# A new instruction order for packed attention with a SoLU layer: weight parts first, score and Z products in one run

## The chip, the cores and the metric

The kernel runs on one core of one Trainium2 chip. The core has TensorE (PE: matrix products into PSUM), VectorE (DVE), ScalarE (ACT), GpSimd (POOL) and SyncE (SP, which here only issues DMAs). The metric is the device time of one execution in microseconds; less is better. Three runs of the kernel before took 371.79 to 372.6 us, median 372.57 us.

## What is computed

```python
s = scale * np.matmul(qq, kk.transpose(0, 1, 3, 2)); s = s - np.max(s, axis=-1, keepdims=True)
a = np.exp(s); a = a / (np.sum(a, axis=-1, keepdims=True) + 1e-09)
sm_attn(qq, kk, vv) = np.matmul(a, vv)
p_packed = sm_attn(p, k, v)              # 32 packed rows per head
x = sm_attn(q, p_packed, p_packed)       # 8 batches, 8 heads, 576 rows, 64 wide
h = x @ w_in                             # (4608, 512) @ (512, 1024)
e = np.exp(h - h_max); sm = e / (np.sum(e, axis=-1, keepdims=True) + 1e-09)
solu = h * sm
ln = (solu - mu) / np.sqrt(var + 1e-06) * g_ln
out = ln @ w_out                         # (4608, 1024) @ (1024, 512)
```

The weights come as 64-bit words and are put together as float32 on the chip before use.

## The kernel before, in words

The work is written as some 1,120 small steps, and a table in the source, `ORDER`, names them in the order in which they are issued. Every engine takes its share of the steps in that order, first in, first out; SP's queue of DMAs too. A step is `name/batch` (attention, eight batches; `/w` for the weights) or `name-tile` (36 tiles of 128 output rows). Behind a colon stands a PSUM bank (0 to 7) or the engine (a = ScalarE, v = VectorE, p = GpSimd) where it can be chosen.

Weights: `lw0` to `lw3` load the four parts of w_in, `lW0` to `lW3` those of w_out, 1024 KB each. `wl` and `wa` take the two halves of each word, `wm` joins them on VectorE (L199). `wp`, `wb`, `pw`, `cs`, `cv`, `ct` find the scales and centre w_out; `ch` and `cl` split it into two float16 halves `wch` and `wcl`; `zw` and `zy` do so for w_in (`w_hi` and the rest). Until a weight part is joined its raw words lie in a buffer that `W_HOME` names.

Attention of a batch: `lk0`, `lk1` (704 and 576 KB), `lv` (1280 KB) and `lq0`, `lq1` (576 KB each) load; `s10`, `s11` are the products of p and K, `mx`, `mb`, `ex` their softmax, `tp`, `tc` (first three batches) or `eh`, `el`, `et`, `ea` the transpose; `av` is the product with V; `pp`, `pt`, `pc` scale and turn it. `sx0`, `sx1` are the scores of q, `sb`, `sm`, `su`, `se`, `ss`, `si`, `sr`, `sn`, `at`, `ah`, `al` their softmax up to the float16 halves `a2h` and `a2l`. `z0`, `z1` multiply the packed rows with w_in (Z = p_packed @ w_in, so that h = a2 @ Z): in float32 for batches below `Z16`, in three float16 terms from there on; `zh`, `zl` split Z into halves. `s1`, `sx` and `z` work on TensorE cut into tiles of 64 rows and 32 columns, `av` into 128 by 32, all others use the whole array.

A row tile i: `m1` is h (12 matmuls of 512 columns), then `nm`, `nb`, `bd`, `ex`, `u`, `mu`, `yh`, `yl`, `sq`, `ca`, `cr` on the other engines, `tr` (a transposing DMA from `yhl` to `yT`), `m2a` and `m2b` (12 matmuls each), `ev` (the scaled copy of the result to `o_sb`) and `st` (the store). Tiles 4, 13, 22 and 31 straddle two batches. An `m1` needs two PSUM banks, which `u` gives back. `m1` of a batch needs that batch's `al` and `zl`.

`hw` are pairs of matmuls whose result nobody reads. After tile 0 to 3 (batch 0) and their second products, the first tile that needs batch 1 follows.

Of the kernel before, what the change touches and what calls it, by code (L numbers as in the profile page):

```python
# [33 lines left out]
se0/0 wa1/w tc0/1:a ss0/0 si0/0:a wa3/w wm1/w hw2/w:1 tc1/1:a wp0/w:6 wp1/w wp2/w tp2/1:2 wl3/w:v sr0/0 sn0/0:p se1/0
wm3/w wp3/w at0/0 wb0/w wb1/w tc2/1:a ss1/0 wb/w z0/0:4 z1/0:0 si1/0:p sr1/0 sn1/0:p wl4/w:a wa4/w wm4/w wa6/w wl6/w:a
ri/1:p un/0 wm6/w ah0/0:a uq/0 wa5/w wl5/w:v wm5/w cs0/w:6 cs1/w wp4/w:7 lk0/2 cs4/w cs5/w cs2/w zh0/0:a zw3/w:p at1/0
cs3/w lk1/2 wp5/w s10/2:2 zl0/0 wl7/w:a wp6/w wa7/w rs/1 zh1/0:a wm7/w mx0/2 ah1/0:a lv/1 wp7/w pw0/w al0/0:p al1/0:p
s11/2:4 pw1/w zl1/0 lq0/1 lq1/1 pw/w mx1/2 cs6/w cs7/w cv/w:a mb0/2:a ko/w gd/w ct0/w ct1/w ct4/w mb1/2:a m1-1:0 ct5/w
nm-1 ex0/2 av/1:7 m1-2:2 lk0/3 bd-1:p ct2/w ex1/2 ri/2:p ch0/w:a pp/1:a ct3/w ct6/w ch2/w:a nb-1:a ch1/w:a cl1/w:p ex-1
ct7/w tp0/2:6 lv/2 nm-2 tc0/2:a bd-2:p u-1 m1-3:4 nm-3 nb-2:a ex-2 u-2 tp1/2:7 cl2/w:p pt/1:6 tc1/2:a pc/1:a yh-1:a  # L40
tp2/2:7 bd-3:p yl-1:p pe/1 s10/3:0 mu-1:a tc2/2:a mx0/3 sq-1 mb0/3:a sx0/1:2 sb0/1 ex0/3 rs/2 ch3/w:a pk/1 un/1 lk1/3
lk0/4 av/2:7 pp/2:v cl0/w:p sx1/1:2 sb1/1 ca-1 nb-3:a s11/3:0 mx1/3 ex-3 mb1/3:a pt/2:6 sm/1 m1-0:2 lq0/2 u-3 nm-0
su/1:p lk1/4 bd-0:p ex1/3 eh/3:a tr-1 lq1/2 yh-3:a yl-3:p nb-0:v z0/1:0 z1/1:4 cl3/w:v cr-1 se/1 tr-3 ss/1 m2a-1:7
zh0/1:a zl0/1 zh1/1:a lk0/5 el/3:p et/3 ex-0 pc/2:a zl1/1 si/1:a sr/1 m2b-1 ev-1:a s10/4:0 s11/4:4 u-0 yh-0:a mx0/4 ca-3
m2a-3:7 sn/1:v pe/2 yl-0:p pk/2 m2b-3 ca-2 mu-3:a mb0/4:a ex0/4 mu-2:a at/1 ah/1:a mx1/4 mb1/4:a al/1:v sx0/2:2 sb0/2
uq/1 sx1/2:0 ex1/4 un/2 sb1/2 ea/3:p ri/4:v m1-4:4 uc-4 nm-4 ri/3:a sm/2 eh/4:a zz/0 el/4:p bd-4:v zw1/w:a sq-3 cr-3
nb-4:v ex-4 yh-2:v yl-2:p mu-0:p sq-2 tr-0 m1-7:2 nm-7 ev-3:a u-4 st-1 ca-0 nb-7:a rs/3 lv/3 ex-7 bd-7:v lk1/5 lq0/3
zy1/w u-7 su/2:p yh-4:a m2a-0:6 mu-7:p m1-8:0 sq-0 cr-0 ca-7 s10/5:4 mx0/5 tr-2 av/3:7 zw2/w:a se/2 nm-8 mb0/5:a bd-8:p
lq1/3 yl-4:p m2b-0 ev-0:a st-3 zy3/w yh-7:a ex0/5 lv/4 m1-6:2 pp/3:v pt/3:7 uq/2 ss/2 si/2:p nm-6 nb-8:a m2a-2:6 ex-8
ca-8 s11/5:4 yl-7:v u-8 mu-8:v cr-2 sq-7 mu-4:a tr-7 sq-4 mx1/5 m2b-2 pe/3 ph/2:a nb-6:a ex-6 pk/3 zy2/w zw0/w:v ev-2:a  # L50
pl/2 zy0/w tr-4 bd-6:p m1-5:0 nm-5 et/4 pc/3:v mb1/5:a ex1/5 u-6 lk0/6 m2a-7:6 lk1/6 yh-8:a st-0 z0/2:4 z1/2:2 zh0/2:a
yl-8:p un/3 ph/3:a sq-8 sr/2 sn/2:v at/2 m2a-4:7 m2b-7 nb-5:a ea/4:v bd-5:p cr-7 m2b-4 uq/3 lk0/7 yh-6:v zh1/2:a zl1/2
sx0/3:2 st-2 mu-6:v ah/2:a al/2:p eh/5:a ex-5 u-5 zz/1 ev-7:a lq0/4 yl-6:p av/4:6 rs/4 zl0/2 sb0/3 sx1/3:0 el/5:p
# [5 lines left out]
yl-9:v sx0/4:2 tr-12 sb0/4 sx1/4:4 sb1/4 sm/4 su/4:v m1-13:0 nm-13 m2a-12:7 bd-13:v nb-13:v m1-11:2 nm-11 m2b-12 ex-13
yh-10:a u-13 yl-10:p sq-10 cr-12 mu-9:a sq-9 nb-11:v ex-11 lq0/5 eh/6:v tr-9 bd-11:v m1-14:4 tr-10 u-11 mu-11:a yh-11:v  # L60
ea/5:p se/4 nm-14 mu-13:a st-5 bd-14:v nb-14:v ex-14 el/6:p m2a-9:6 rs/5 yl-11:p lq1/5 av/5:0 pp/5:a ev-12:v m1-16:2
pe/5 cr-9 u-14 nm-16 m2b-9 m1-17:0 ca-11 m2a-10:7 et/6 nb-16:v st-12 ss/4 ph/4:a yh-13:v yl-13:v lv/6 nm-17 bd-17:v
tr-11 sq-13 ca-13 cr-13 sq-11 cr-11 ex-16 cr-10 lq0/6 bd-16:p m1-15:4 m2b-10 st-8 zz/2 tr-13 nb-17:v u-16 ex-17 u-17
si/4:v ev-10:a ca-17 pl/4 ea/6:v sr/4 sn/4:p ev-9:a st-9 z0/4:2 yh-16:v z1/4:0 at/4 st-10 zh0/4:a zl0/4 zh1/4:a zl1/4
m2a-11:7 mu-16:v pt/5:6 m2b-11 yl-16:v uq/4 ca-16 sq-16 cr-16 m2a-13:0 ev-11:a nm-15 nb-15:v tr-16 lk1/7 ah/4:v bd-15:p
ex-15 u-15 mu-15:v yh-15:v yl-15:p pk/5 al/4:v mu-17:p m2b-13 pc/5:v un/5 uq/5 m2a-16:7 st-11 rs/6 sx0/5:2 sq-15 ev-13:a
sx1/5:4 yh-14:v sb0/5 s10/7:0 s11/7:2 av/6:6 mx0/7 mb0/7:p sb1/5 sm/5 yl-14:p mu-14:a sq-14 tr-15 uc-22 m1-20:4 mx1/7
pp/6:a pe/6 pt/6:6 yh-17:a nm-20 ph/5:a lq1/6 pl/5 m2b-16 ex0/7 zz/3 mb1/7:a st-13 nb-20:a tr-14 m1-19:0 ex1/7 su/5:v
bd-20:p ex-20 u-20 pc/6:a se/5 ss/5 si/5:p pk/6 z0/5:2 z1/5:4 ev-16:a m2a-14:7 un/6 zh1/5:a ca-14 cr-14 nm-19 m2a-15:6
eh/7:a ca-15 el/7:p m2b-14 m2b-15 sr/5 bd-19:p sn/5:v at/5 ah/5:a zh0/5:v al/5:v zl0/5 zl1/5 m1-23:2 lv/7 et/7 yh-20:a  # L70
ev-14:a st-14 mu-20:p yl-20:v ea/7:v sx0/6:4 cr-15 yl-17:p tr-17 av/7:7 sq-20 sb0/6 nb-19:a ex-19 u-19 m1-22:4 nm-23
nb-23:v ev-15:a st-15 bd-23:p ri/7:a rs/7 pp/7:v sq-17 ex-23 sx1/6:0 nm-22 sb1/6 m2a-17:6 ca-19 ca-20 u-23 yh-23:v
mu-23:v tr-20 m2a-20:7 cr-20 nb-22:a yl-23:p sm/6 m1-24:0 nm-24 ex-22 ca-23 m2b-20 m1-21:2 bd-22:p m2b-17 sq-23 tr-23
# [826 lines left out]
```

## Time and profile before

| | us |
|---|---|
| median of three runs | 372.57 |
| the profiled execution | 372.9 |
| its span, first to last instruction | 371.1 |
| PE busy | 354.9 (96%) |
| DVE busy | 278.9 (75%) |
| ACT busy | 209.1 (56%) |
| POOL busy | 214.7 (58%) |

The profiled execution is 1.8 us longer than its span, and 0.33 us longer than the median. Busy times are sums over a program with unlike stages: the loads and the weights up to about 46 us, a stage up to about 80 us in which w_out is still being split while tiles 0 to 3 run, and the long rest. Matmul rows begin every 0.216 us where TensorE does not wait, though each lasts 0.38 us, since they are pipelined.

### The profile page before, as it was taken

The numbers are of one execution on the slowest core, as the hardware profiler recorded it, in microseconds if no ns is written. First come the engines' busy times: TensorE is split into PE (matmuls) and PEld (weight loads), VectorE is DVE, ScalarE is ACT, GpSimd is POOL, SyncE is SP. The second block draws the span as 40 slices with busy tenths as digits, with TensorE's granted clock in tenths as the row PEclk, the third lists the DMA queues.
The fourth block names the chain that finished last, engine by engine and source line by source line (L and its number), as shares of the span: only waits on it lengthen the run. The fifth ranks groups of instructions, "written<-read, shape, count | busy, mean of one in ns | idle before, by whom it ended". The sixth has DMA issues, their size and how long they took to land.

```text
span 371.1 us, 7650 instructions
## 1 busy us (share of the span) xinstructions
PE 354.9 (96%) x3027; PEld 165.9 (45%) x3027; DVE 278.9 (75%) x421; ACT 209.1 (56%) x357; POOL 214.7 (58%) x304
## 2 busy tenths in 40 slices
...
GB/s 284 425 422 419 425 382 68 126 266 284 229 191 325 227 171 157 153 150 258 156 212 171 198 115 124 44 97 150 148 115 164 92 113 59 113 141 54 148 170 58
DMA packets 99349, 70.57 MB, mean 190 GB/s; under 512 B 88048, under 2 KB 88048, under 8 KB 97776
## 3 DMA queue, kind: packets, MB, share of 16 engines
...
q8 instruction: 24, 0.39, 0.4%
q14 instruction: 13, 0.11, 0.1%
HBM read 38.80 MB, written 9.44 MB: 130 GB/s over the span
## 4 chain that ended last, share of the span: by engine, by line
PE 83%; DVE 7%; DMA 6%; POOL 3%; issue 1%; ACT 0%; SPq 0%; POOLq 0%
PE pa L789 41%; PE ps L723 23%; PE ps L789 8%; DMA qT<-in_q_dram 4%; PE ps L604 3%; PE ps L538 2%; PE pa L316 1%; PE pa L504 1%; DMA zh<-in_moe_w_in_dram 1%; POOL wcl L329 1%; PE ps L436 1%; DVE u L752 1%; DVE zl L622 1%; DVE nm L729 1%; DVE yT L323 1%; POOL s L586 1%
## 5 line engine op out<-in xcount | busy, mean ns | idle before, releaser
L789 PE MATMUL pa<-wch,yT 128*128 128x512 f16 x480 | 149.5, 379 | 0.8 <-ACT yhl L148 0.8
L789 PEld LDWEIGHTS <-yT 128*128 128x128 f16 x864 | 83.2, 98 | 104.5 <-issue 4.8
L789 PE MATMUL pa<-wcl,yT 128*128 128x512 f16 x240 | 91.0, 379 | 0.0
L729 DVE TENSOR_REDUCE nm<-ps 128x1 f32<-128x1024 f32 x36 | 43.9, 1220 | 29.1 <-PE ps L723 28.9
L763 POOL TENSOR_TENSOR yhl<-u,yhl 128x1024 f16<-128x1024 f32 x23 | 51.2, 2227 | 21.2 <-ACT yhl L148 9.8
L747 ACT ACTIVATE e<-ps,bias,unit 128x1024 f32<-128x1024 f32 x36 | 43.3, 1202 | 35.4 <-DVE bias L144 28.5
L723 PE MATMUL ps<-zh,a2h 128*128 128x512 f16 (+1 forms) x160 | 54.8, 380 | 0.1
L752 DVE SCALAR_TENSOR_TENSOR u<-e,s_row,ps 128x1024 f32<-128x1024 f32 x36 | 45.6, 1267 | 12.2 <-ACT e L747 9.6
L723 PE MATMUL ps<-zh,a2l 128*128 128x512 f16 (+1 forms) x160 | 54.6, 379 | 0.0
L723 PE MATMUL ps<-zl,a2h 128*128 128x512 f16 (+1 forms) x160 | 54.6, 379 | 0.0
L771 ACT ACTIVATE e<-u,negmu 128x1024 f32<-128x1024 f32 x36 | 41.1, 1143 | 8.0 <-DVE negmu L144 7.8
L723 PEld LDWEIGHTS <-a2h 128*128 128x128 f16 (+1 forms) x320 | 27.7, 100 | 33.9 <-issue 3.1
L740 POOL TENSOR_SCALAR bound<-nm,unit 128x1 f32<-128x1 f32 x22 | 18.9, 859 | 27.1 <-DVE nm L729 27.0
L789 PE MATMUL ps<-wch,yT 128*128 128x512 f16 x96 | 30.2, 379 | 0.0
L142 ACT ACTIVATE o_sb<-pa,c_row 128x512 f32<-128x512 f32 x22 | 14.9, 684 | 25.9 <-POOL c_row L782 9.2
L148 ACT CAST yhl<-u 128x1024 f16<-128x1024 f32 x20 | 20.7, 1041 | 15.3 <-DVE u L752 13.0
L781 POOL TENSOR_SCALAR c_row<-sq,k_out,s_eps 128x1 f32<-128x1 f32 x36 | 14.8, 411 | 20.1 <-ACT e L771 19.4
L782 POOL TENSOR_TENSOR c_row<-c_row,neg_half 128x1 f32<-128x1 f32 x36 | 22.3, 619 | 3.0
L775 POOL TENSOR_SCALAR s_eps<-se,s_row 128x1 f32<-128x1 f32 x36 | 14.5, 402 | 15.3 <-ACT e L747 12.2
L723 PEld LDWEIGHTS <-a2l 128*128 128x128 f16 (+1 forms) x160 | 14.3, 100 | 16.8
L763 DVE TENSOR_TENSOR yhl<-u,yhl 128x1024 f16<-128x1024 f32 x13 | 17.6, 1354 | 2.3 <-ACT yhl L148 2.2
L789 PE MATMUL ps<-wcl,yT 128*128 128x512 f16 x48 | 18.2, 379 | 0.0
...
## 6 DMA issues: line engine op xcount, KB each, us to landing
...
```

The source lines that it names most:

```text
L142: nc.scalar.activation(out, in_, AF.Copy, scale=scale)
L148: nc.scalar.copy(out, in_)
L723: nc.tensor.matmul(h[rows, 512 * n:512 * n + 512], lhsT=lhsT, rhs=z[:, r, 512 * n:512 * n + 512], start=t == 0, stop=t == end)
L729: nc.vector.tensor_reduce(out=nm, in_=st['h'], axis=AX.X, op=ALU.max, negate=True)
L740: eng.tensor_scalar(out=bound, in0=st['nm'], scalar1=st['nm'], scalar2=st['unit'][:, 2:3], op0=ALU.mult, op1=ALU.max)
L747: nc.scalar.activation(st['e'], st['h'], AF.Exp, bias=st['bias'], scale=st['unit'][:, 1:2], accum_out=st['se'])
L752: nc.vector.scalar_tensor_tensor(out=st['u'], in0=st['e'], scalar=st['s_row'], in1=st['h'], op0=ALU.mult, op1=ALU.mult, accum_out=st['su'])
L763: engines[on(f'yl-{i}', 'v')].tensor_tensor(out=st['y'][:, 1], in0=st['u'], in1=st['y'][:, 0], op=ALU.subtract)
L771: nc.scalar.activation(st['e'], st['u'], AF.Square, bias=st['negmu'], accum_out=st['sq'])
L781: nc.gpsimd.tensor_scalar(out=c_row, in0=st['sq'], scalar1=k_out[:, 0:1], scalar2=s_eps, op0=ALU.mult, op1=ALU.add)
L782: nc.gpsimd.tensor_tensor(out=c_row, in0=c_row, in1=neg_half, op=ALU.pow)
L789: nc.tensor.matmul(st['po'], lhsT=st['yT'][:, a, c], rhs=w[:, c], start=c == 0 and t == 0, stop=c == NFC - 1 and t == 2)
```

## The change

The table `ORDER` is new as a whole, with 1,115 steps in place of 1,120. Beside it four edits stand:

```diff
-Z16 = 2
+Z16 = 3
-W_HOME = 'zh zl zh zl kT qT v zh'.split()
+W_HOME = 'zh w_hi zh wcl kT qT v wch'.split()
     def stage(home):
-        if home in ('zh', 'zl'):
+        if home in ('w_hi', 'wcl', 'wch'):
+            return {'w_hi': w_hi, 'wcl': wcl, 'wch': wch}[home].rearrange('p a b -> p (a b)').bitcast(I32)
+        if home == 'zh':
...
-            st['y'] = mlp.tile([P, 2, DF], F16, name='yhl', bufs=2)
+            st['y'] = mlp.tile([P, 2, DF], F16, name='yhl', bufs=3)
...
-            st['yT'] = mlp.tile([P, 2, NFC, P], F16, name='yT', bufs=2)
+            st['yT'] = mlp.tile([P, 2, NFC, P], F16, name='yT', bufs=3)
...
         def output():
             st['o'] = mlp.tile([P, DM], F32, name='o_sb', bufs=2)
-            scaled(on(f'ev-{i}', 'a'), st['o'], st['po'], st['c'])
+            if i == B * S // P - 1:
+                for eng, cols in (('a', slice(0, DM // 2)), ('v', slice(DM // 2, DM))):
+                    scaled(eng, st['o'][:, cols], st['po'][:, cols], st['c'])
+            else:
+                scaled(on(f'ev-{i}', 'a'), st['o'], st['po'], st['c'])
```

The third batch's Z is thus made in float32, in two passes over w_in as it stands, and `zw` and `zy` are moved behind it. Three raw parts are put where split weights will stand later. Row parts and their transposes have three buffers, and the copy of the last tile listed is done in two halves by two engines. In the table one line of before and one of after:

```diff
-lg/w hw1/w:6 lw0/w hw25/w:7 gx/w wa0/w wl0/w:v wm0/w lw2/w wa2/w wl2/w:a lk0/0 hw9/w:6 s10/0:0 mx0/0 lk1/0 s11/0:2
+hw47/w:6 lw3/w wa3/w lw1/w wl1/w:a hw29/w:7 lk0/0 hw22/w:6 s10/0:0 mx0/0 lk1/0 wl3/w:v s11/0:2 hw23/w:7 mx1/0 lv/0
```

SP's queue of loads at the start, before (w_in's parts go to `zh` and `zl`):

```order
L157 DMA g_sb<-in_moe_g_ln_dram 128x8
L167 DMA zh<-in_moe_w_in_dram 128x2048 x2
L411 DMA kT<-in_k_dram 128x1408
L411 DMA kT<-in_k_dram 128x1152
L411 DMA kT<-in_k_dram 128x1408
L420 DMA v<-in_v_dram 128x2560
L411 DMA kT<-in_k_dram 128x1152
L416 DMA qT<-in_q_dram 128x1152 x2
L167 DMA zl<-in_moe_w_in_dram 128x2048 x2
L167 DMA kT<-in_moe_w_out_dram 128x2x1024
```

The same queue after:

```order
L169 DMA wcl<-in_moe_w_in_dram 128x2048
L169 DMA w_hi<-in_moe_w_in_dram 128x2048
L413 DMA kT<-in_k_dram 128x1408
L413 DMA kT<-in_k_dram 128x1152
L422 DMA v<-in_v_dram 128x2560
L169 DMA zh<-in_moe_w_in_dram 128x2048
L413 DMA kT<-in_k_dram 128x1408
L413 DMA kT<-in_k_dram 128x1152
L418 DMA qT<-in_q_dram 128x1152
L169 DMA zh<-in_moe_w_in_dram 128x2048
L418 DMA qT<-in_q_dram 128x1152
L169 DMA kT<-in_moe_w_out_dram 128x2x1024
```

The third and fourth part of w_in stand ahead of half or all of q of batch 0 now, V ahead of the second batch's K, and the gains behind w_out's first parts.

VectorE in the opening, before (`u<-zl` is `wl`, `w_in_sb` is `wm`, `s`, `mx`, `sm` are the softmax of batch 0's scores, `w_peak` the first step to w_in's scale):

```order
L563 TENSOR_REDUCE mx<-s_294 128x18
L560 STREAM_TRANSPOSE s_294<-ps_76 128x576
L563 TENSOR_REDUCE mx<-s_294 128x18
L188 TENSOR_SCALAR u<-zl 128x1024
L572 TENSOR_REDUCE sm<-s_294 128x18
L199 SCALAR_TENSOR_TENSOR w_in_sb<-e,u 128x1024
L188 TENSOR_SCALAR u<-zl 128x1024
L583 RECIPROCAL sm<-sm 128x18
L199 SCALAR_TENSOR_TENSOR w_in_sb<-e,u 128x1024
L627 STREAM_TRANSPOSE s_386<-s_294 128x576
L211 TENSOR_REDUCE w_peak_388<-pa_79 128x1
```

VectorE at the same work after:

```order
L201 SCALAR_TENSOR_TENSOR w_in_sb<-e,u 128x1024 x3
L467 RECIPROCAL rs<-ssum 128x2
L442 TENSOR_REDUCE nmx<-ps_78 128x1
...
L562 STREAM_TRANSPOSE s_303<-ps_76 128x576
L190 TENSOR_SCALAR u<-zh 128x1024
L565 TENSOR_REDUCE mx<-s_303 128x18
L201 SCALAR_TENSOR_TENSOR w_in_sb<-e,u 128x1024
L562 STREAM_TRANSPOSE s_303<-ps_78 128x576
L467 RECIPROCAL rs<-ssum 128x2
L565 TENSOR_REDUCE mx<-s_303 128x18
L213 TENSOR_REDUCE w_peak_379<-pa_80 128x1
```

Three parts of w_in are joined ahead of the scores, one behind them; the two `mx` and the second transpose have moved behind the last `wl`.

TensorE around batch 5's first score product, before (it stands alone, with `av` behind it):

```order
L723 MATMUL ps_76<-zl,a2h_108 128x512
L723 LDWEIGHTS a2l_109
L723 MATMUL ps_76<-zh,a2l_109 128x512
L436 MATMUL ps_78<-kT 32x288 x8
L504 MATMUL pa_80<-v,e1T 32x64 x40
L789 LDWEIGHTS yT
L789 MATMUL pa_79<-wch,yT 128x512
```

TensorE at that product after:

```order
L791 MATMUL pa_79<-wch,yT 128x512
L540 MATMUL ps_77<-qT,ppT 32x288 x8
L540 MATMUL ps_76<-qT,ppT 32x288 x8
L606 MATMUL ps_78<-w_in_sb,ppT 32x512 x8
L438 MATMUL ps_77<-kT 32x288 x8
L438 MATMUL ps_76<-kT 32x288 x8
L791 LDWEIGHTS yT
```

Both scores of q, half of a Z and both products of K follow one another. Counted in the table from `sx1/2` on, products on 64 by 32 tiles stood in 14 separate runs and stand in 10; with `av` counted in, the whole array is returned to 14 times before and 12 times after.

## Rows read from the trace of the kernel before

**Rows 1.** Stages: length, busy us of PE, PEld, DVE, ACT, POOL; clock, DMA share, GB/s.

```profile
10.00:20.00 10.00, 8.08 (x173) 3.90 (x173) 4.96 (x10) 4.52 (x11) 0.00 (x0) 0.83 1.02 425
24.61:46.67 22.06, 18.11 (x157) 8.82 (x155) 19.12 (x41) 15.01 (x19) 14.60 (x11) 0.92 1.02 421
46.67:79.10 32.43, 30.62 (x398) 14.69 (x397) 31.66 (x46) 29.18 (x57) 28.13 (x27) 1.00 0.64 199
80.00:110.00 30.00, 30.00 (x284) 13.68 (x276) 27.13 (x43) 22.41 (x39) 27.79 (x34) 1.00 0.84 245
```

**Rows 2.** TensorE's waits from 37 to 340 us: us, times, longest.

```profile
PE pa L789 <- ACT yhl L148: 0.8, 1, 0.8
...
PE ps L538 <- ACT negmu L142: 0.4, 1, 0.4
```

**Rows 3.** TensorE in order of time: Z of batches 0 and 1, `m1-1`, `m1-4`.

```profile
31.94 3.62 PE L604 MATMUL ps<-w_in_sb,ppT 64*32 64x512 f32 x32
46.39 0.38 PE L723 MATMUL ps<-zh,a2h 128*128 128x512 f16 x1
65.04 1.95 PE L604 MATMUL ps<-w_in_sb,ppT 64*32 64x512 f32 x32
80.63 0.41 PE L723 MATMUL ps<-zh,a2h 128*64 128x512 f16 x2
```

**Rows 4.** ScalarE on w_in's first and last part; SP's first load.

```profile
6.17 1.16 ACT L182 ACTIVATE e<-zh 128x1024 f32<-128x1024 f32 x1 [3.96 <-DMA zh<-in_moe_w_in_dram]
27.04 1.17 ACT L182 ACTIVATE e<-zl 128x1024 f32<-128x1024 f32 x1 [0.61 <-DMA zl<-in_moe_w_in_dram]
0.72 0.39 SPq L157 DMA_DIRECT2D g_sb<-in_moe_g_ln_dram  x1
```

**Rows 5.** VectorE in order of time: `mx`, `wl`, `wm` twice, the scale's end, `al/1`.

```profile
21.21 0.75 DVE L563 TENSOR_REDUCE mx<-s 128x18 f32<-128x576 f32 x1
24.61 0.69 DVE L188 TENSOR_SCALAR u<-zl 128x1024 int32<-128x1024 int32 x1
25.88 1.52 DVE L199 SCALAR_TENSOR_TENSOR w_in_sb<-e,u 128x1024 int32<-128x1024 int32 x1
28.24 1.23 DVE L199 SCALAR_TENSOR_TENSOR w_in_sb<-e,u 128x1024 int32<-128x1024 int32 x1
46.44 0.23 DVE L299 TENSOR_SCALAR gs<-g_sb,w_scale 128x8 f32<-128x8 f32 x1
77.75 1.36 DVE L639 TENSOR_TENSOR a2l<-s,a2h 128x1152 f16<-128x1152 f32 x1 [0.58 <-ACT a2h L148]
```

**Rows 6.** TensorE on the chain that ended last: start, us, matmuls.

```profile
109.83 1.44 PE ps L604 x48
...
119.14 0.65 PE ps L538 x16
...
269.82 1.13 PE ps L538 x32
...
272.26 2.70 PE ps L789 x12
274.96 2.59 PE pa L789 x12
```

**Rows 7.** ScalarE's last copy, in order of time.

```profile
367.46 0.69 ACT L142 ACTIVATE o_sb<-pa,c_row 128x512 f32<-128x512 f32 x1 [4.49 <-PE pa L789]
```

**Rows 8.** Copies of 128 by 256 by engine: count, busy us, mean ns, idle before.

```profile
L148 ACT COPY ppT<-pa 128x256 f32<-128x256 f32 x5 | 1.8, 369 | 2.5 <-PE pa L520 2.5
...
L150 DVE COPY ppT<-pa 128x256 f32<-128x256 f32 x2 | 0.8, 414 | 0.0
```

**Rows 9.** GpSimd beside VectorE's `wm` of 25.88 us, in order of time.

```profile
24.75 1.56 POOL L566 TENSOR_TENSOR s<-s,mx 128x576 f32<-128x576 f32 x1 [1.54 <-DVE mx L563]
```

**Rows 10.** VectorE's `yl` by its line: shortest, median, longest ns.

```profile
L763 DVE TENSOR_TENSOR yhl<-u,yhl x13: 1181/1224/2675, 99.7 to 354.4; 128x1024 f16<-128x1024 f32 x13
```

**Rows 11.** One microsecond of batch 0's Z, columns as in rows 1.

```profile
32.00:33.00 1.00, 1.00 (x17) 0.38 (x24) 0.86 (x6) 0.95 (x1) 0.22 (x1) 0.50 1.05 430
```

More of the change, by code (lines that the diff above doesn't have):

```diff
@@ L34 @@
[L34 to L53, printed above, removed]
@@ L59 @@
[L59 to L73, printed above, removed]
```

97 lines of the change are left out of this document (66 added, 31 removed).

## The prediction

> **What bounds the kernel now.** I read the stages first, then TensorE's waits, then each engine in order of time at the places where the stages change. From 80 us TensorE is busy 30.00 of 30.00 us, and between 37 and 340 us it waits three times only, from 0.8 down to 0.4 us, 1.7 us in all [rows 1, 2]. So the end is the time at which that unbroken stretch gets going, plus the products still to be made, plus the tail behind the last product. What sets the start of the stretch is seen in two stages before it. From 24.61 us, where VectorE takes up the third part of w_in, to 46.67 us, where w_out's scale is done, VectorE is busy 19.12 of 22.06 us; from there to 79.1 us 31.66 of 32.43 us [rows 1, 5]. VectorE is thus the bound from the weights' landing to `al/1` of batch 1, which it ends at 77.75 + 1.36 = 79.11 us. The first tile that needs `al/1`, `m1-4`, begins at 80.63 us [rows 3]: TensorE came to it 1.5 us after it could have, because it still had other products in its row.
>
> **The change part by part.** Terms are differences. They are made against the profiled execution (span 371.1, own time 372.9 us) and hold for the median, which is 0.33 us less.
>
> *The loads.* Readers of w_in's first and last part begin at 6.17 and 27.04 us [rows 4]; by the table of loads 8064 KB lie between, 386 KB a microsecond. DMA is full here (share 1.02), so another order moves landings and not the sum. In the new queue the third part (the first into `zh`) ends after 5632 KB, 6.17 + 4608/386 = 18.1 us; the last after 8512 KB, 25.6 us; q's second half takes the place of w_in's last part, 27.0 us. The gains' load no longer stands first and took 0.39 us of SP's queue; I credit nothing for it and keep 0.4 us for the range. Behind w_in the sum of bytes is as before, so w_out's last part lands when it did.
>
> *VectorE up to w_out's scale.* Before, two parts were joined after 24.61 us; now three are joined before the last lands, in a stage where VectorE is busy 4.96 of 10 us [rows 1]. That takes one `wl` and one `wm` out of the bound stretch: 0.69 + 1.23 = 1.92 us [rows 5]. Three operations on batch 0's scores come in, since they now stand behind the last `wl` (two `mx`, 0.75 us [rows 5]; a transpose of the same tile, 0.75 us by estimate from that row), and two tiny ones on the gains, 0.3 us at most: 2.55 us. So 19.12 - 1.92 + 2.55 = 19.75 us of work from 25.6 us on. Without a gap it ends at 45.35 us, 1.3 us earlier than before; with all the 2.94 us that VectorE stood idle before (22.06 - 19.12) at 48.3 us, 1.6 us later. I take 0.5 us of idle, because in the new row other work stands ahead of the steps that GpSimd or TensorE must finish first: 45.8 us, 0.9 us earlier.
>
> *ScalarE in the same stage.* Two copies of batch 0's transposed softmax now stand behind the third part's `wa`, so they wait for 18.1 us, and `av/0`, `sx0/0` with them. That costs nothing while q's second half lands only at 27.0 us, since `sx1/0` needs it anyway; if it is late it moves VectorE's `mx` one for one.
>
> *From there to the first tile of batch 1.* The steps between are nearly the same set, VectorE has 0.8 us of idle in 32.43 us [rows 1], so I carry the 0.9 us over: `al/1` at 78.2 us. TensorE must have made by then what it had made before 80.63 us: tiles 0 to 3, two `m2`, the same scores and Z (the new row puts tile 7 in the place of tile 4). That took 80.63 - 46.39 = 34.2 us with 1.7 us of waits [rows 2, 3], 32.5 us without. From a start 0.9 us earlier, 45.5 us, it is there at 78.0 us, just ahead of `al/1`. So the stretch begins at 78.2 in place of 80.63 us: **-2.4 us**. The bounds: without any idle in the stage before -1.3 - 1.5 = -2.8 us (-3.2 with the 0.4 us of SP's queue); with all of it +1.6 - 1.5 = +0.1 us.
>
> *TensorE's products behind it.* Z of batch 2 in float32 takes 1.95 us [rows 3], in three float16 terms 1.44 us [rows 6]: +0.5 us. A run of 64 by 32 tiles has a cost of its own: one `sx` alone 0.65 us, two together 1.13 us, 2 x 0.65 - 1.13 = 0.17 us for one run fewer; and the first full-array product behind a run takes 2.70 and not 2.59 us, 0.11 us [rows 6]. Four runs and two returns fewer: 4 x 0.17 + 2 x 0.11 = 0.9 us. Together **-0.4 us**; if runs of unlike kinds save nothing, +0.5 us.
>
> *The tail.* The last copy takes 0.69 us [rows 7]; copies of half the size take 0.37 us on ScalarE and 0.41 us on VectorE [rows 8], side by side: **-0.3 us**, at worst 0, if the store waits for the later half. The three unread pairs of matmuls behind the last product ran beside that copy; taking them out is worth nothing.
>
> *Edits at nothing.* The third buffer for `yhl` and `yT` lets a transpose start earlier; TensorE waits for none after 75 us, so there is nothing to win. The raw parts' new homes add no instruction. `zw` and `zy` (eight operations) stand between batch 2's Z and batch 3's; VectorE has 2.9 us free in 30 from 80 us on, ScalarE 7.6 us [rows 1], which covers them; without that cover each would cost TensorE its own 1.2 us or so (an estimate from the `wm`, an operation of the same size [rows 5]).
>
> Sum: -2.4 - 0.4 - 0.3 = -3.1 us: 369.8 us in the profiled execution, **369.5 us** for the median. Its own range is 368.4 (-3.2 - 0.4 - 0.3, and 0.3 us, since one execution is read that lies 0.33 us off the median) to 371.2 us (half the opening's gain lost).
>
> **Rivals.**
>
> *The earlier start is given back.* VectorE's idle stays as long as before or longer, since `wm` of w_out's parts, `ss` and `sr` now wait for ScalarE in another order. Then the opening gives +0.1 us and only the other two terms stay: 372.57 + 0.1 - 0.4 - 0.3 = 372.0 us. For it: all `wa` and three of four `wl` of w_out are ScalarE's. Against it: it is busy 15.01 of 22.06 us in that stage [rows 1].
>
> *GpSimd stops VectorE, and it gets slower.* The `wm` of 25.88 us, which reads two tiles from SBUF, took 1.52 in place of 1.23 us, and ended its hold-up where GpSimd's subtraction ended, 24.75 + 1.56 = 26.31 us [rows 5, 9]; a `yl` took 2.675 us where the median is 1.224 [rows 10]. So a meeting of two such operations costs up to 1.45 us. The new table gives GpSimd more of them: four more `yl`, two more `ea`, two more `su`, one more `al` and `cl`, one `sn` fewer. GpSimd is busy 28.13 of 32.43 us up to 79.1 us already, and 27.79 of 30 after it [rows 1]. From the third meeting up to 110 us that other work doesn't cover, the gain is gone with the 0.8 us of idle: three give 372.57 - 3.1 + 3 x 1.45 = 373.8 us. Against it: the median of VectorE's `yl` lies close to its shortest, 1.181 us [rows 10], so most meetings are short or don't happen. The Trainium skill ("SBUF — State Buffer", section "SBUF: two separate sides") states this as a rule: GpSimd and a VectorE operation with two inputs from SBUF share one pair of ports, and whichever starts first holds it for the whole instruction. By that rule this rival is certain in kind, and only the count of meetings is open; the row of 25.88 us agrees, with 0.3 us of delay.
>
> *A low clock on the path, or a late half of Z.* Batch 0's Z ran at a granted clock of 0.50 [rows 11], the lower level of 1.2 GHz, and took 3.62 us where batch 1's took 1.95 at 2.4 GHz [rows 3]: 1.7 us. The unread pairs now all stand ahead of batch 1's scores, so TensorE is idler ahead of that Z. If the clock is low later, between 38 and 45 us where TensorE is on the path too, 1.7 us of the opening's gain go: 371.2 us. Z of batch 2 made in two places, the second half some 9 us ahead of its first tile, costs about as much if `ah/2` and `al/2` are late.
>
> That the runs of small tiles don't join as meant is no rival of its own: it costs 0.9 us, 370.4 us, inside my range.
>
> **How the numbers follow.** Forecast 0.60; given back 0.18; slower by meetings 0.11; clock or late Z 0.11. A measurement can tell 0.3%, 1.12 us: faster is below 371.45, slower above 373.69 us. Faster: 0.59 of the forecast, 0.08 of the last case, 0.05 of the case given back, 0.72. Same: 0.01 + 0.13 + 0.03 = 0.17. Slower: 0.11. The range of 368.4 to 372.6 us leaves out the slower case and the far ends of two others, 0.19 in all.
>
> **What would show it.** In the profile after, w_out's scale (the steps before the first `ct`) ends near 45.8 us, `al/1` near 78.2, and TensorE starts tile 7 at once behind it and waits for nothing later. The float32 Z of batch 2 shows as rows of 0.9 us a half; scores and Z that stand together show 2.59 us products with fewer 2.70 us ones. The tail from the last product to the end is 0.3 us shorter. I am wrong if the scale ends after 46.7 us, if tile 7 begins after 80 us, or if TensorE shows waits of a microsecond between 80 and 130 us; `yl`, `sn` or `al` of 2 us and more on VectorE there would name GpSimd.

## The result, and the profile of the changed kernel

The changed kernel takes **375.9 us** (median), the kernel before 372.6 us in the same runs: ratio 1.009, 95% interval 1.0074 to 1.0106. It was forecast 3.1 us faster, and it is 3.3 us slower. The profiled executions, 374.4 and 371.1 us of span, lie as far apart, so the difference can be read from them.

TensorE is the engine to add up. In both kernels the same set of products stands ahead of `m1-1`, so I take the stretch from there to the end of the last product. The stretch in the kernel before: its length, then TensorE's busy time (the columns of [rows 1]).

```profile
46.39:367.39 321.00, 319.18 (x2640) 146.66 (x2639) 249.44 (x364) 182.42 (x317) 197.96 (x281) 1.00 0.61 162
```

The same in the changed kernel:

```profile
45.19:370.70 325.51, 320.27 (x2623) 147.16 (x2621) 242.37 (x350) 186.17 (x322) 208.59 (x290) 1.00 0.62 160
```

The stretch begins 1.20 us earlier, its products take 320.27 - 319.18 = 1.09 us more, and TensorE stands idle for 325.51 - 320.27 = 5.24 us in place of 1.82, 3.42 us more. Behind it 374.4 - 370.7 = 3.7 us follow, as before (371.1 - 367.39). Sum: -1.20 + 1.09 + 3.42 = +3.3 us. So the opening kept its promise up to there, and what was lost is **waits of TensorE that the forecast had at nothing**. They are these, up to 340 us (who waited for whom: us in total, times, longest):

```profile
PE ps L725 <- DVE a2l L641: 1.5, 2, 1.0
PE pa L791 <- DMA yT<-yhl: 1.3, 1, 1.3
PE ps L540 <- DMA qT<-in_q_dram: 1.3, 1, 1.3
```

The rest are six of 0.13 to 0.25 us; [rows 2] had three waits in all. (Line numbers are two higher than before in most of the kernel: L725 is `m1`, L791 `m2`, L540 `sx`, L641 `al`.)

The opening is where it was forecast. VectorE's scale of w_out ends at 45.53 us (46.67 before, [rows 5]), and Z of batch 0, at the low clock in [rows 3, 11], now takes what batch 1's took (VectorE and TensorE of the changed kernel in order of time):

```profile
45.30 0.23 DVE L301 TENSOR_SCALAR gs<-g_sb,w_scale 128x8 f32<-128x8 f32 x1
29.73 1.95 PE L606 MATMUL ps<-w_in_sb,ppT 64*32 64x512 f32 x32
```

Then the place on which the forecast rested. VectorE's `al/1`, GpSimd's `yl-2` and `ea/3` beside it, and TensorE's tile 7, which needs `al/1` from its third matmul on (the changed kernel in order of time: start, us, in brackets the idle time ahead and what ended it):

```profile
77.40 3.47 DVE L641 TENSOR_TENSOR a2l<-s,a2h 128x1152 f16<-128x1152 f32 x1
75.18 2.14 POOL L765 TENSOR_TENSOR yhl<-u,yhl 128x1024 f16<-128x1024 f32 x1
77.27 2.37 POOL L497 TENSOR_TENSOR e1T<-eT 128x1152 f32<-128x1152 f16 x1
79.31 0.39 PE L725 MATMUL ps<-zh,a2h 128*128 128x512 f16 x1
80.92 0.39 PE L725 MATMUL ps<-zh,a2l 128*128 128x512 f16 x1 [1.00 <-DVE a2l L641]
```

`al/1` takes 3.47 where it took 1.36 us [rows 5]. It was issued 0.13 us behind `ea/3`, and it ends 1.23 us behind `ea/3`'s end (79.64 us): as if it had begun only then.

### The profile page after: what moved, and what is told of

Its sections match the earlier page's. It is cut to its first block, busy times and chain, and to the rows that moved or that the text cites. A ratio compares the mean times of both kernels' runs of the same rounds, so it can differ in the third digit from the quotient of the medians.

```text
span 374.4 us, 7602 instructions
## 1 busy us (share of the span) xinstructions
PE 353.5 (94%) x3005; PEld 165.8 (44%) x3005; DVE 271.3 (72%) x407; ACT 212.6 (57%) x362; POOL 220.8 (59%) x312
## 4 chain that ended last, share of the span: by engine, by line
PE 70%; DVE 11%; DMA 10%; ACT 4%; POOL 2%; issue 1%; SPq 0%; ACTq 0%; POOLq 0%; DVEq 0%
PE pa L791 30%; PE ps L725 20%; PE ps L791 15%; DMA zh<-in_moe_w_in_dram 5%; DMA yT<-yhl 3%; DVE a2l L641 2%; DMA w_hi<-in_moe_w_in_dram 2%; PE ps L606 2%; DVE nm L731 2%; PE ps L540 1%; DVE mx L565 1%; DMA qT<-in_q_dram 1%; PE ps L438 1%; PE pa L318 1%; DVE s L562 1%
## 5 line engine op out<-in xcount | busy, mean ns | idle before, releaser
L791 PEld LDWEIGHTS <-yT 128*128 128x128 f16 x864 | 83.4, 98 | 105.2 <-issue 5.0
L791 PE MATMUL pa<-wch,yT 128*128 128x512 f16 x400 | 124.6, 379 | 1.5 <-DMA yT<-yhl 1.3
L791 PE MATMUL pa<-wcl,yT 128*128 128x512 f16 x200 | 75.8, 379 | 0.0
L765 POOL TENSOR_TENSOR yhl<-u,yhl 128x1024 f16<-128x1024 f32 x27 | 59.8, 2220 | 26.6 <-ACT yhl L148 18.0
L725 PE MATMUL ps<-zh,a2l 128*128 128x512 f16 (+1 forms) x160 | 55.7, 379 | 1.5 <-DVE a2l L641 1.5
L791 PE MATMUL ps<-wch,yT 128*128 128x512 f16 x176 | 55.5, 379 | 0.2 <-DVE pp L144 0.2
L725 PE MATMUL ps<-zh,a2h 128*128 128x512 f16 (+1 forms) x160 | 55.4, 380 | 0.3 <-DVE zl L624 0.2
L725 PE MATMUL ps<-zl,a2h 128*128 128x512 f16 (+1 forms) x160 | 55.3, 379 | 0.0
L725 PEld LDWEIGHTS <-a2h 128*128 128x128 f16 (+1 forms) x320 | 28.2, 100 | 34.2 <-issue 2.7
L742 POOL TENSOR_SCALAR bound<-nm,unit 128x1 f32<-128x1 f32 x24 | 15.7, 656 | 43.1 <-DVE nm L731 34.2
L791 PE MATMUL ps<-wcl,yT 128*128 128x512 f16 x88 | 33.4, 379 | 0.0
L148 ACT CAST yhl<-u 128x1024 f16<-128x1024 f32 x25 | 25.7, 1040 | 13.4 <-DVE u L754 8.9
L142 ACT ACTIVATE bias<-nm,unit 128x1 f32<-128x1 f32 x25 | 7.3, 292 | 42.0 <-DVE nm L731 41.8
L725 PEld LDWEIGHTS <-a2l 128*128 128x128 f16 (+1 forms) x160 | 14.8, 100 | 19.1 <-DVE a2l L641 2.5
L568 POOL TENSOR_TENSOR s<-s,mx 128x1152 f32<-128x1152 f32 (+1 forms) x7 | 13.9, 1981 | 12.3 <-DVE mx L565 12.2
L442 DVE TENSOR_REDUCE nmx<-ps 128x1 f32<-128x576 f32 x16 | 11.8, 749 | 10.8 <-PE ps L438 10.8
```

The lines of the kernel that those rows point to most:

```text
L148: nc.scalar.copy(out, in_)
L568: by('su', x).tensor_tensor(out=part(st['w'], x), in0=part(st['w'], x), in1=spread(st['mx'], x), op=ALU.subtract)
L725: nc.tensor.matmul(h[rows, 512 * n:512 * n + 512], lhsT=lhsT, rhs=z[:, r, 512 * n:512 * n + 512], start=t == 0, stop=t == end)
L742: eng.tensor_scalar(out=bound, in0=st['nm'], scalar1=st['nm'], scalar2=st['unit'][:, 2:3], op0=ALU.mult, op1=ALU.max)
L765: engines[on(f'yl-{i}', 'v')].tensor_tensor(out=st['y'][:, 1], in0=st['u'], in1=st['y'][:, 0], op=ALU.subtract)
L791: nc.tensor.matmul(st['po'], lhsT=st['yT'][:, a, c], rhs=w[:, c], start=c == 0 and t == 0, stop=c == NFC - 1 and t == 2)
```

## The experiments

Each kernel ran beside the kernel before; its ratio is to that. Start, products and waits are TensorE's, read as above from each profiled execution; of the kernels that aren't in the table the ratio stands in the text.

| kernel | ratio (95%) | start | products | waits |
|---|---|---|---|---|
| before | 1 | 46.39 | 319.2 | 1.8 |
| changed | 1.0090 (1.0074 to 1.0106) | 45.19 | 320.3 | 5.2 |
| e8_again | 1.0077 (1.0062 to 1.0091) | 45.51 | 320.0 | 3.8 |
| e1_apart | 1.0036 (1.0019 to 1.0053) | 45.23 | 319.9 | 3.6 |
| e2_q_load | 1.0090 (1.0059 to 1.0122) | 45.25 | 319.8 | 5.0 |
| e5_k_later | 1.0033 (1.0017 to 1.0048) | 45.11 | 319.9 | 3.2 |
| e6_k4_later | 1.0067 (1.0043 to 1.0091) | 45.43 | 319.9 | 4.2 |
| e10_q_ahead | 0.9984 (0.9970 to 0.9998) | 45.13 | 319.3 | 2.1 |
| e12_ea_back | 1.0024 (1.0004 to 1.0044) | 45.14 | 319.5 | 3.7 |
| e13_opening3 | 0.9992 (0.9981 to 1.0002) | 45.39 | 319.1 | 2.0 |

**Two operations that meet.** The theory: a GpSimd and a VectorE operation that each read two inputs from SBUF shut each other out. One token of the row is moved:

```diff
-yl-2:p rs/3 sq-3 mu-0:a ea/3:p ca-3 cr-3 sq-2
+yl-2:p rs/3 sq-3 mu-0:a ca-3 cr-3 ea/3:p sq-2
```

> The changed kernel, but GpSimd's `ea/3` (2.37 us) stands behind `ca-3` and `cr-3` in its row, so that it doesn't begin beside VectorE's `al/1`, which took 3.47 us there in place of 1.36. Theory (the two operations shut each other out, GpSimd's first): `al/1` takes about 1.4 us and ends near 78.8 in place of 80.87 us, TensorE's wait of 1.01 us ahead of tile 7's low part is gone with the 0.16 us that its restart costs, and the time is 1.0 to 1.2 us shorter, 374.8 us. Rival 1 (`al/1` is long because of the transpose by DMA that begins at 77.34 us, which stays where it is): `al/1` stays at 3.4 us, 375.9 us. Rival 2 (the delay is covered later): `al/1` is short again and the time stays within 0.4 us, since TensorE then waits as much longer for q's load at 146 us.

It came out as the theory has it, and by more than was forecast: 1.0036, 2.0 us below the changed kernel as first measured and 1.5 us below e8_again. VectorE's `al/1` and GpSimd's row in e1_apart, in order of time:

```profile
77.24 1.36 DVE L641 TENSOR_TENSOR a2l<-s,a2h 128x1152 f16<-128x1152 f32 x1
77.49 1.24 POOL L777 TENSOR_SCALAR s_eps<-se,s_row 128x1 f32<-128x1 f32 x1
80.22 2.37 POOL L497 TENSOR_TENSOR e1T<-eT 128x1152 f32<-128x1152 f16 x1
```

The transpose by DMA beside it (rival 1) still began at 77.4 us. The changed kernel itself, unedited, then gave the best proof.

> The changed kernel as it is, on the chip of these runs, so that the others have a standard beside them. Expected: 375.9 us, `al/1` of 3.2 to 3.5 us, and a wait of about 1 us for it ahead of tile 7.

This expectation failed, to the theory's gain. In e8_again's profiled execution `al/1` was ready a quarter of a microsecond ahead of `ea/3`, and now `ea/3` was the long one (VectorE and GpSimd of e8_again in order of time; the row between them is `yl-2`):

```profile
77.28 1.51 DVE L641 TENSOR_TENSOR a2l<-s,a2h 128x1152 f16<-128x1152 f32 x1
75.44 2.13 POOL L765 TENSOR_TENSOR yhl<-u,yhl 128x1024 f16<-128x1024 f32 x1
77.53 3.49 POOL L497 TENSOR_TENSOR e1T<-eT 128x1152 f32<-128x1152 f16 x1
```

TensorE had no wait ahead of tile 7, and its last product ended at 369.32 in place of 370.70 us. One program, two outcomes: whoever starts first holds the other up, and which one that is, by 0.13 us or by 0.25, was not the same in these two executions.

The delay has a measure. `yl-2` ended at 75.44 + 2.13 = 77.57 us here, and `al/1`, issued 0.29 us before that, ended 1.22 us behind it; in the changed kernel it ended 1.23 us behind `ea/3`. In the traces of before, the changed kernel, e1_apart, e10_q_ahead and e12_ea_back a two-input operation of GpSimd was first eleven times beside an `al` of VectorE, and each of these `al` ends 1.21 to 1.23 us behind GpSimd's operation, whenever it was issued. One of them is `al/3` of the changed kernel, beside `yl-11` (VectorE and GpSimd):

```profile
150.80 2.95 DVE L641 TENSOR_TENSOR a2l<-s,a2h 128x1152 f16<-128x1152 f32 x1
150.39 2.14 POOL L765 TENSOR_TENSOR yhl<-u,yhl 128x1024 f16<-128x1024 f32 x1
```

Another, `al/4` at 193 us, takes 2.86 us, and behind it TensorE waits 0.18 us at most; it stays in e10_q_ahead. So a meeting cost the kernel time only where TensorE was close behind. The last run on this puts `ea/3` back into the best version (e10_q_ahead, below).

```diff
-yl-2:p rs/3 sq-3 mu-0:a ca-3 cr-3 ea/3:p sq-2
+yl-2:p rs/3 sq-3 mu-0:a ea/3:p ca-3 cr-3 sq-2
```

> e10_q_ahead, with one of its three moves undone: `ea/3` stands on GpSimd right behind `yl-2` again, so that it and `al/1` become ready within 0.3 us of each other. Theory (whichever starts first holds the other up for its whole length): in executions where `ea/3` is first `al/1` takes about 3.4 us, TensorE waits 0.8 to 1.0 us ahead of tile 7, and the time is 1.0 to 1.2 us above e10_q_ahead, 373.4 us; where `al/1` is first it is 372.3 us; the times fall into two groups or spread by more than those of e10_q_ahead (371.5 to 372.7 us). Rival (the meeting is covered now that the later waits are gone): 372.2 us in all of them.

Two groups: three executions at 371.8, 372.1 and 372.6 us, nine from 373.8 to 374.4 us; those of e10_q_ahead lie between 371.5 and 372.7 us. That the groups differ by who was first is not shown: only one execution was profiled, and e3_three (below), with `ea/3` moved away, has five from 372.3 to 372.9 us and the others from 374.0 us on. The profiled one is of the second group, with e12_ea_back's VectorE, GpSimd and TensorE as follows:

```profile
77.53 3.22 DVE L641 TENSOR_TENSOR a2l<-s,a2h 128x1152 f16<-128x1152 f32 x1
77.17 2.37 POOL L497 TENSOR_TENSOR e1T<-eT 128x1152 f32<-128x1152 f16 x1
80.81 0.39 PE L725 MATMUL ps<-zh,a2l 128*128 128x512 f16 x1 [0.76 <-DVE a2l L641]
```

From e10_q_ahead to here the ratio rises by 1.5 us (0.9984 to 1.0024), but not all of that is the meeting. In the profiled executions tile 7 already begins 0.60 us later here (79.44 and 78.84 us), since TensorE's wait for `tr-1` at 64 us was 1.47 and not 0.86 us, long before `ea/3` was issued. What comes after is 1.28 us of a total of 1.88, and 0.76 us of it is the wait shown.

**Loads and transposes in one queue.** TensorE's wait at 146 us is for q's load `lq1/4`. SyncE's own row in the changed kernel shows why it is late (issue start, and how long the issue held SyncE):

```profile
129.40 4.09 SPq L493 DMA_TRANSPOSE eT<-eh  x1
133.62 8.67 SPq L769 DMA_TRANSPOSE yT<-yhl  x3
142.38 0.53 SPq L802 DMA_DIRECT2D out_dram<-o_sb  x1
142.96 0.42 SPq L418 DMA_DIRECT2D qT<-in_q_dram  x1
```

Four transposes and a store stand ahead of it, and the transposes hold the queue for 13 us. First the load was moved far ahead (here and below, the place that a token leaves is not always shown):

```diff
-rs/4 lq0/4 m2b-4 yh-5:a zy0/w
+rs/4 lq0/4 lq1/4 m2b-4 yh-5:a zy0/w
```

> The changed kernel, but the load `lq1/4` is issued right behind `lq0/4` (near 117 us) and not at 142.96 us behind three transposes. Theory (the load's place in SP's row alone costs TensorE the wait of 1.26 us at 146 us, 0.16 us for the restart, and pushes the next steps so that `al/3` meets `yl-11`): no wait there, and 1.3 to 2.1 us less, 374.2 us. Rival (TensorE would wait there anyway, for the transposed softmax's steps or for the next tile's `al/3`, and the wait only moves): less than 0.5 us, 375.6 us.

The rival was right: no gain (1.0090). The load came in time, but `et/5` behind it was now held 6.69 us, and TensorE waited for a transpose at 140 us instead, and at 146.5 us 0.42 us for a copy. SyncE's row in e2_q_load:

```profile
129.44 6.69 SPq L493 DMA_TRANSPOSE eT<-eh  x1
```

TensorE in e2_q_load, in order of time:

```profile
140.47 0.39 PE L791 MATMUL pa<-wch,yT 128*128 128x512 f16 x1 [0.89 <-DMA yT<-yhl]
```

e3_three joined this with `ea/3` moved and `yl-11` ahead of `uq/3`.

> The changed kernel with `ea/3` behind `cr-3`, `lq1/4` behind `lq0/4`, and `yl-11` ahead of `uq/3` on GpSimd (it began 0.4 us before `al/3`, which took 2.95 us, and TensorE waited 0.53 us for it). Theory (three separate costs that add): 1.2 + 1.4 + 0.7 = 3.3 us less, 372.6 us, the kernel before again. Rival (they hide each other; the first late step behind the last cure takes the gain): under 2 us less, 374 us or more, with new waits of TensorE between 150 and 230 us.

Its rival came nearer: 1.0038 (1.0010 to 1.0066), 1.9 us less than the changed kernel and no better than e1_apart alone. Then k's loads were moved, out of the way of the four transposes:

```diff
-zz/1 yl-6:v ph/3:a lk0/7 nm-9 nb-9:v
+zz/1 yl-6:v ph/3:a nm-9 nb-9:v
-mu-9:a lk1/7 et/5 bd-11:p
+mu-9:a et/5 bd-11:p
-yl-10:v tr-10 cr-5
+yl-10:v tr-10 lk0/7 lk1/7 cr-5
```

> The kernel with `ea/3` behind `cr-3` (e1_apart), and the loads `lk0/7` and `lk1/7` (1280 KB) issued behind `tr-10`, near 162 us, and not at 123 us ahead of four transposes; their reader `s10/7` stands near 180 us. In e1_apart the transposes `et/5`, `tr-6`, `tr-5`, `tr-9` behind the loads took SyncE 2.4 to 3.5 us each to issue, where most of this kernel's take 1.6, and q's load `lq1/4` behind them came 1.12 us late for TensorE at 144 us. Theory (k's loads in front make the transposes slow, and these make q's load late): the four issues come down towards 1.6 to 2 us, q's load is issued 2 us or more earlier, TensorE's wait is gone, and with the restart and the wait for `al/3` behind it 1.2 to 1.7 us go: 372.8 us against 374.3. Rival (the transposes are slow for another reason): issues of 2.4 to 3.5 us as before, within 0.4 us of e1_apart.

The theory fell for three of the four: `et/5` was issued in 1.85 us (2.66 in e1_apart), but the three behind it held the queue for 10.65 us (9.80), q's load was issued only 0.5 us earlier, and TensorE still waited 1.06 us. The ratio, 1.0033, is that of e1_apart. In all four kernels with k's loads moved `et/5` is issued in 1.85 to 1.91 us, in the four with them in front (and q's load where it was) in 2.66 to 4.26 us. Loads in flight are thus one cause of a slow transpose, and not the only one. The next kernel asked the same of `tr-1`.

```diff
-un/1 lq0/2 lq1/2 lk0/4 lk1/4 yl-1:p tr-1
+un/1 lq0/2 lq1/2 yl-1:p tr-1 lk0/4 lk1/4
```

> e5_k_later, and the loads `lk0/4` and `lk1/4` issued behind `tr-1`, near 62 us, in place of 44 and 46 us. `tr-1` took SyncE 3.2 to 3.7 us to issue and TensorE waited 1.1 to 1.5 us for it at 62.6 us, though the last load in front had landed 0.8 us earlier. Theory (the loads in front make it slow): issue near 1.7 us, no wait of TensorE at 62.6 us; TensorE is then ahead of `al/1`, which ends at 78.6 us, and only about 0.5 us of it remain as gain, if k comes in time for `s10/4` at 69 us. Rival (it is the first transpose of the program or what runs beside it): issue above 3 us again, the wait stays, no gain; and if the loads land after 69 us it gets slower by as much.

Again the rival: `tr-1` is as slow as before, and `tr-3`, behind the loads now, takes 4.70 us to issue where it took 1.58. The ratio rises to 1.0067. SyncE's row in e6_k4_later:

```profile
58.49 3.46 SPq L769 DMA_TRANSPOSE yT<-yhl  x1
62.05 0.99 SPq L413 DMA_DIRECT2D kT<-in_k_dram  x2
64.37 4.70 SPq L769 DMA_TRANSPOSE yT<-yhl  x1
```

What helped was to let the load pass one transpose only, the last, which has time to spare (and `yl-11` no longer meets `al/3`):

```diff
-pp/4:a pe/4 tr-9 st-7 s11/6:0
+pp/4:a pe/4 lq1/4 tr-9 st-7 s11/6:0
-z1/3:4 mu-12:p m2a-9:2
+z1/3:4 mu-12:p yl-11:p m2a-9:2
```

> e5_k_later, with q's load `lq1/4` issued right ahead of the transpose `tr-9` in place of behind it, and `yl-11` ahead of `uq/3` on GpSimd, so that it ends before `al/3` begins. In e5_k_later TensorE waited 1.06 us for this load and 0.49 us for `al/3`. Theory (both waits go and nothing else is late by then, since `tr-9`, even at 8 us, lands 2 us ahead of its reader): 1.06 + 0.49 + 2 x 0.16 = 1.9 us less, 371.6 us against 373.5, below the kernel before. Rival (as with e2_q_load, a load in flight makes the transposes behind it slow and the wait only moves): less than 0.7 us, with a wait for a transpose between 135 and 155 us.

As expected: 0.9984, 1.8 us below e5_k_later, and below the kernel before by 0.6 us; the interval (0.9970 to 0.9998) just leaves out no difference. SyncE's row in e10_q_ahead has q's load 7.8 us earlier:

```profile
135.17 0.58 SPq L418 DMA_DIRECT2D qT<-in_q_dram  x1
136.62 2.85 SPq L769 DMA_TRANSPOSE yT<-yhl  x1
```

Its TensorE waits up to 340 us for these:

```profile
PE pa L791 <- DMA yT<-yhl: 0.9, 1, 0.9
PE ps L725 <- DVE unit L254: 0.5, 1, 0.5
PE pa L476 <- ACT e1T L148: 0.2, 1, 0.2
PE ps L725 <- DVE zl L624: 0.2, 1, 0.2
```

**The opening by itself.** The changed kernel's opening, up to the first `m1`, was put in front of the row of the kernel before. The first two tries, e9_opening (1.0072) and e11_opening2 (1.0081), tell nothing on it: at the seam `m1-1` waited 2.76 us for a bank and 3.13 us for `al1/0`. They show what a wait of that size at the head of the stretch is worth: nearly all of it, at the end.

> The opening of the changed kernel (its row up to the first `m1`, with its homes of the raw weights, its three buffers and its halved copy of tile 35) and from there the row of the kernel before, with Z of batch 2 in float16 as there. It separates the opening's gain from the rest of the new row. In the changed kernel w_out's scale ended at 45.5 us, in the kernel before at 46.67 us. Theory (the prediction's carry is right as long as no operation of GpSimd begins beside `al/1`): `al/1` takes 1.4 us and ends near 78.1 in place of 79.11 us, `m1-4` begins near 79.5 in place of 80.63 us, and the time is 0.9 to 1.2 us below the kernel before, 371.3 us against 372.4. Rival 1 (the earlier start is given back by VectorE's waits before `al/1`, whatever the row behind it): 372.4 us, with VectorE's idle time up by 1 us. Rival 2 (loads that now stand at other times slow the transposes behind 55 us): slower than before, with TensorE's waits for transposes.

> The question of e9_opening again: the opening of the changed kernel, then the row of the kernel before with Z of batch 2 in float16. There `m1-1` had to wait 2.76 us, since at the seam it took a PSUM bank that batch 2's scores still held; here the banks 0, 1 and 4, 5 are exchanged behind the seam, and `zw3`, `uq/0`, `ko` and `gd` stand behind the same steps as in the kernel before. Theory (the carry holds as long as no operation of GpSimd begins beside `al/1`): `m1-1` at 45.2 us, `al/1` of 1.4 us that ends near 78.1, `m1-4` near 79.5 us, and 0.9 to 1.2 us below the kernel before, 371.5 us against 372.6. Rival 1 (given back by VectorE's waits before `al/1`): `al/1` ends at 78.8 us or later and the time is that of the kernel before within 0.4 us. Rival 2 (loads that stand at other times slow the transposes behind 55 us): slower than before.

The third has no wait there.

> e11_opening2 with `uq/0`, `ko` and `gd` behind `al1/0` on GpSimd, as in the changed kernel, so that `m1-1` waits for nothing at the seam. Theory (the carry holds where no operation of GpSimd begins beside `al/1`): `m1-1` at 45.4 us and running on, `al/1` of 1.4 us that ends between 78.1 and 78.5 us, `m1-4` at 79.5 us, and 0.9 to 1.2 us below the kernel before. Rival 1 (given back by VectorE's waits ahead of `al/1`): `al/1` ends at 78.8 us or later, the kernel before within 0.4 us. Rival 2 (loads at other times slow the transposes behind 55 us): slower than before by over 0.5 us.

In the trace the theory holds: `al/1` ends at 78.27 us, 0.84 us earlier than in [rows 5], `m1-4` begins at 79.84 us, 0.79 us earlier than in [rows 3], and the last product ends 0.88 us earlier. VectorE's `al/1` and TensorE's `m1-4` in e13_opening3:

```profile
76.91 1.36 DVE L641 TENSOR_TENSOR a2l<-s,a2h 128x1152 f16<-128x1152 f32 x1 [0.57 <-ACT a2h L148]
79.84 0.41 PE L725 MATMUL ps<-zh,a2h 128*64 128x512 f16 x2
```

The stretch from `m1-1` to `m1-4` in e13_opening3 (columns as above):

```profile
45.39:79.84 34.45, 32.43 (x434) 15.32 (x432) 32.27 (x50) 30.70 (x58) 30.60 (x34) 1.00 0.69 213
```

The same in the kernel before:

```profile
46.39:80.63 34.24, 32.43 (x432) 15.34 (x431) 32.22 (x49) 30.45 (x59) 29.73 (x32) 1.00 0.67 205
```

By the runs the gain is at the edge of what they tell: 0.9992 (0.9981 to 1.0002), between 0.7 us faster and 0.1 slower. And TensorE comes to `m1-4` 1.57 us behind `al/1`, as before: it waits 2.02 us in that stretch, before 1.81.

**Z of batch 2, and the halved copy.** e7_z_f32 is the kernel before with `Z16 = 3`, without `ph/2` and `pl/2`, and with the four `zy` moved:

```diff
-Z16 = 2
+Z16 = 3
```

> The kernel before, but Z of batch 2 is made in float32; `ph/2` and `pl/2` are gone, and the four `zy` stand behind that Z, one each behind `sm/3`, `mx1/6`, `nm-9` and `nm-10`. The prediction's term: 1.95 in place of 1.44 us of TensorE, 0.5 us slower, 373.0 us against 372.5. Rival 1 (the price is about 1.0 us, as the sum of Z's rows grew by 0.98 us in the changed kernel): 373.5 us. Rival 2 (VectorE, with its four `zy` later, holds up TensorE between 110 and 140 us): over 1 us slower and waits of TensorE there.

TensorE's own price is as forecast. Z of batch 2 in the kernel before (stretch, length, TensorE's busy time in that line alone):

```profile
108.00:113.00 5.00, 1.51 (x48) 0.61 (x48) 1.00 1.05 238
```

In e7_z_f32:

```profile
108.00:113.00 5.00, 1.95 (x32) 0.49 (x32) 1.00 1.02 243
```

Its two halves in the changed kernel:

```profile
86.00:92.00 6.00, 1.09 (x16) 0.18 (x16) 1.00 0.11 44
108.00:113.00 5.00, 1.06 (x16) 0.31 (x16) 1.00 1.37 201
```

That is +0.44 us in one piece and +0.64 in two. But the whole was 1.024 (1.0217 to 1.0263), 9 us slower, and rival 2 was right: where I put the `zy`, VectorE came late for a row that wasn't drawn for it. Behind two of them (126.75 and 129.58 us) TensorE waited 1.45 us for VectorE and then 1.88 us for ScalarE, which had waited for VectorE. A third wait of 1.3 us, for a transpose at 217 us, is far from them, and its cause stays open. Since the placement is mine, no price of the edit follows from it, except TensorE's.

e4_tail halves the copy of tile 31, the last in the row, where the changed kernel halves that of tile 35, which begins 5 us earlier (365.60 and 370.78 us; the tile's products ended at 360.3 us, 10 us ahead of the last ones):

```diff
-            if i == B * S // P - 1:
+            if i == 31:
```

> The changed kernel, but the copy that is halved is that of tile 31, which is the last in the row; in the changed kernel it is that of tile 35, whose products end 15 us ahead of the end. Theory (the term of the prediction was right and stood at the wrong tile): the copy of 0.69 us becomes two of about 0.4 us side by side, 0.3 us less, 375.6 us. Rival (the store waits for the later half, and it begins late): no difference, 375.9 us.

Neither theory nor rival: the halves don't run side by side. ScalarE's and VectorE's half in e4_tail:

```profile
370.73 0.47 ACT L142 ACTIVATE o_sb<-ps,c_row 128x256 f32<-128x256 f32 x1 [1.57 <-PE ps L791]
371.23 0.48 DVE L144 TENSOR_SCALAR o_sb<-ps,c_row 128x256 f32<-128x256 f32 x1 [1.27 <-ACT o_sb L142]
```

VectorE waits for ScalarE, so the copy ends 1.07 us behind the last product (370.64) where one whole copy ends 0.78 us behind it (370.69 to 371.47): 0.3 us longer. In the changed kernel VectorE's half of tile 35 waited for ScalarE's too. Whether the wait comes from the output tile or from the PSUM bank that both share wasn't tried. The ratio, 1.0064 (1.0036 to 1.0091), can't tell 0.3 us from e8_again.

## Why the prediction was wrong, step by step

- **The loads and the opening: right.** The scale ended at 45.53 (45.8 forecast), Z of batch 0 ran at the full clock and in time. The rival of the low clock fell.
- **The carry of 0.9 us to `al/1`: right in the old row, half right in the new.** It was 0.84 us in e13_opening3. In the changed row `al/1` began only 0.35 us earlier, since VectorE's idle time ahead of it grew by 0.6 us (1.40 and 0.77 us), and in e1_apart, where nothing holds it up, it ends 0.51 us earlier. The rival of the start given back was right to that extent.
- **TensorE "is there at 78.0 us": wrong, and 1.5 of the forecast 2.4 us.** I took the measured 34.2 us, subtracted its 1.7 us of waits, and let nothing take their place. The products were sized right (32.47 us in the changed kernel, 32.5 forecast), but the waits stayed: 1.65 us in the changed kernel (1.28 of it for `tr-1`), 2.02 in e13_opening3, where they are the three of [rows 2] again (0.89, 0.72 and 0.33 us, all ended by ScalarE). The forecast named nothing that would take them away, and nothing did. What makes `tr-1` late stays open: e6_k4_later's cure failed, and e10_q_ahead still waits 0.86 us for it.
- **`al/1` at 1.36 us: wrong; the rival of the meetings was right in kind and mis-sized.** I gave it 0.11, with a price of up to 1.45 us each and three meetings needed. It took one on the path, of 2.11 us, and a smaller one at `al/3` (1.6 us longer, 0.53 us of TensorE's wait). Against it I had set the median of all `yl` [rows 10], which says how often two operations meet somewhere. What mattered was what GpSimd does at the one place where `al/1` starts, and that the new row showed: `yl-2` and `ea/3` back to back. In the kernel before it was a near miss. Its `yl-0` on GpSimd ended at 77.72 us, and `al/1` began at 77.75 [rows 5]:

```profile
75.58 2.14 POOL L763 TENSOR_TENSOR yhl<-u,yhl 128x1024 f16<-128x1024 f32 x1
```

  The Trainium skill ("SBUF — State Buffer", section "SBUF: two separate sides") has the rule that the first to start holds the shared ports for its whole instruction. The traces agree with it in both directions: `al/1` of 3.47 us in the changed kernel and 3.22 in e12_ea_back, `ea/3` of 3.49 us in e8_again, and 1.36 and 2.37 us in e1_apart, where they don't meet.
- **TensorE "waits for nothing later": wrong.** The row of SyncE was counted in bytes and not in the time for which an issue holds the queue. q's load behind four transposes cost 1.26 us, and its cure with `yl-11`'s was worth 1.8 us (e5_k_later to e10_q_ahead).
- **TensorE's products at -0.4 us: mis-sized, and mostly through the waits.** They measured +1.09 us; in e10_q_ahead, where the waits are nearly gone, the same products take 319.25 us, +0.07. So about 1 us came with the waits. Of the rest Z costs 0.64 us (0.5 forecast); by subtraction the joined runs of small tiles would save 0.64 - 0.07, 0.6 us (0.9 forecast), but no run shows that term by itself.
- **The tail at -0.3 us: wrong.** The halved copy is not the last one, and the last one, halved, takes longer: the halves don't run side by side.
- **The range.** Its upper end, 371.2 us, doesn't follow from what stands beside it: with half of the 2.4 us lost the sum gives 370.7 us, and 371.0 with the 0.3 us of the lower end.

The sum: forecast -0.9 (start), -1.5 (TensorE's waits), -0.4, -0.3; measured -1.20, +3.42, +1.09, 0.0. With `ea/3`, k's loads, q's load and `yl-11` moved, e10_q_ahead is below the kernel before: the slowdown came from these places in the new order and not from the order as a whole. But the forecast 3.1 us aren't there either. In e10_q_ahead's profile the same sum is -1.26, +0.26, +0.07, 0.0: only the earlier start is left as a gain.
